# A two-step attention cycle with mixed score/maximum pairs, single-bank exponentials, and V, raw outputs and row maxima through DRAM

## The chip, the cores and the metric

One core of a Trainium2 chip. The metric is device microseconds of one execution. Engines: TensorE (PE) multiplies matrices into PSUM (eight banks of 128 partitions x 512 fp32), VectorE (DVE), ScalarE (ACT) and GpSimd (POOL) work on tiles, SP's queue issues most DMAs. Each engine runs its instructions in the order of its queue and waits on semaphores of the others.

## The reference

Two rounds of (multi-head attention block, then a dense block with Mish), each on a layer norm and added to x; all in fp32.

```python
B, S, D, H = 1, 2048, 512, 32        # head width 16; dense width F = 1792
def A(x, wqkv, wo):
    q, k, v = split(x @ wqkv)                    # [H, S, 16] each
    p = softmax(einsum("hqd,hkd->hqk", q, k) * 16 ** -0.5)
    return merge(einsum("hqk,hkd->hqd", p, v)) @ wo
def Bk(x, w1, b1, w2):
    h = x @ w1 + b1
    return (h * tanh(softplus(h))) @ w2
x = x + A(ln(x)); x = x + Bk(ln(x)); x = x + A(ln(x)); x = x + Bk(ln(x))
```

## The kernel before

Precision: where fp32 accuracy is wanted from fp32r matmuls, an operand is split in a high and a low part (`split_load`, `split_psum`), and `mm3` issues three matmuls for each product. Q and K are stacked in the partitions so that one matmul over 48 rows holds high and low parts (`KROWS`); two more rows (`MROWS` = 50) carry the negative row maximum in high and low parts against rows of ones in K. So a score matmul gives q.k - max directly, and the exponential needs no other operand. Even heads use partitions 0 to 49, odd heads 64 to 113 (`HALF`).

Stages, for each of two layers: q, k, v (`qkv`; q and k go to DRAM tiles `scr` and come back by head), attention, the output projection (`wo_parts`), the dense block (`mlp`). Attention runs over 8 groups of 4 heads; in a group over 4 blocks of 512 queries; in a block over 16 steps of 128 keys: 512 steps a layer, 32 blocks. A step has

- four score matmuls 50x128 by 50x512, into `sp` (two banks, two heads, item P, `pair`) or `ss` (one bank, item S, `single`), and the exponential of each PSUM tile into `p` (L312 for a pair, 1024 columns; L322 for a single, 512 columns);
- four maximum matmuls (item M twice, `max_mm`, tile `pm` of two banks for two heads) for a block that is 24 steps ahead (`AHEAD`), and for each M one reduction over 1024 columns on DVE (L265, tile `mxv`);
- two pv items (item v, `pv`, L339): half of the queries each, four heads side by side in the columns of the array, added up over the block in the bank `acc`. A fp32 matmul shows as two records here.

Every three steps follow the same cycle, and TensorE's instructions in attention are chained in that order (`pe`):

```python
CYCLE = ("PMSvv", "PMSvMPMSv", "PMSvvM")
```

At the end of a block of maxima DVE folds them (`max_fold`, L272, tile `nm`); TensorE transposes the fold (`nmt`), DVE splits it (`np`, L284 and L285), and eight DMAs on SP (L289) put the rows into the Q tiles `qs`. At the end of a block of pv ACT drains the bank (`ot`, L356); TensorE transposes it (`otp`), DVE takes the reciprocal of the sums and multiplies (`rc`, `o`, L367 and L368) into `ost`, four tiles that stay in SBUF. The four V tiles of a layer stay in SBUF too, and POOL builds from them the tile `va` of each group (L232 to L235). All these, the tiles of Q, K, `p` and the weights share one pool, `blk`, of 22 slots. PSUM: `pm` has two buffers of two banks, `sp` one of two banks, `ss` one, `acc` one.

The last 24 steps have no M items left; there the projection of the first 512 rows (`wo_parts`, transposes `op`, matmuls `wo`) is put between the steps. The weights `wo` and the first four tiles of w1 are loaded in the last group and split by POOL.

## Time and profile before

| | us |
|---|---|
| runs shown | 3944.41, 3948.99, 3965.48 (median 3948.99) |
| profiled execution, span | 3965.9 |
| first norm, q, k, v of layer 0 | 0 to 202 |
| attention, layer 0 | 202 to 1648.5 |
| rest of the projection, dense block, q, k, v of layer 1 (overlapping) | 1648.5 to 2194 |
| attention, layer 1 | 2194 to 3601.8 |
| rest of the projection, dense block | 3601.8 to 3966 |

The profiled execution's span stands at the time of the slowest of the three runs. In rows of stretches the columns are: start and end, length, then busy time and count for PE, PE's weight loads, DVE, ACT, POOL (with a filter on a line: that line's engine alone), the granted share of the TensorE clock, the busy share of the DMA engines, GB/s. In rows of the order of time: start, duration from the first to the last of the merged instructions, engine, line, operation, tiles, count, and in brackets the idle time before and what ended it. A TensorE record's duration counts its latency, so neighbours overlap; the distance of starts tells what one costs.

### The profile page before, as it was taken

What the parts mean: (1) busy time and instruction counts of PE and PEld (TensorE: products, weight loads), DVE (VectorE), ACT (ScalarE), POOL (GpSimd) and SP (SyncE); (2) the same over time, 40 slices, a digit from 0 to 9 for tenths busy, and PEclk for the clock granted to TensorE, in tenths of its full rate; (3) what the DMA queues carried; (4) which work ended last, traced back from release to release, by engine and by line L of the source; (5) the groups of instructions that cost most, each with busy time, mean ns of one, the idle gap of its engine ahead of it and who ended that gap; (6) DMA issues with size and microseconds to landing.
All of it is one profiled execution on the core that took longest, in us unless ns stands there. A gap on an engine that the chain in (4) does not pass through costs nothing.

```text
span 3965.9 us, 70422 instructions
## 1 busy us (share of the span) xinstructions
PE 3802.0 (96%) x29504; PEld 2090.7 (53%) x29504; DVE 3093.7 (78%) x3266; ACT 2517.8 (63%) x3445; POOL 494.2 (12%) x401
## 2 busy tenths in 40 slices
PE   7999999999999999999999999999999999999999
PEld 5744444444444444588776444444444444446887
DVE  5689989687988898466656799897998979965655
ACT  2177777576776777544431777776777767774444
POOL 1000000000000011254420000000000000204545
PEclk9999999697998999999999999998999989999999
DMA  6220111110010201100033201111110202101000
GB/s 186 107 34 10 26 18 18 17 18 18 18 28 8 34 12 44 53 7 22 22 123 128 34 7 29 18 18 18 18 30 6 34 2 34 34 23 59 11 11 22
DMA packets 65326, 134.58 MB, mean 34 GB/s; under 512 B 12272, under 2 KB 26608, under 8 KB 58864
## 3 DMA queue, kind: packets, MB, share of 16 engines
q1 hardware_dynamic: 42768, 89.17, 10.6%
q10 hardware_dynamic: 22240, 40.90, 2.9%
q8 instruction: 232, 3.80, 0.4%
q14 instruction: 86, 0.70, 0.1%
HBM read 85.99 MB, written 41.94 MB: 32 GB/s over the span
## 4 chain that ended last, share of the span: by engine, by line
PE 44%; DVE 4%; ACT 2%; POOL 1%; DMA 1%; issue 1%; POOLq 0%; DVEq 0%; ACTq 0%; SPq 0%
PE pv L339 13%; PE pm L261 9%; PE sp L311 6%; PE ss L321 4%; DVE mxv L265 2%; PE mo L133 1%; PE h L131 1%; PE h L133 1%; PE h L132 1%; PE mo L131 1%; PE mo L132 1%; ACT p L312 1%; POOL hb L532 1%; DVE al L533 1%; PE qk L131 1%
## 5 line engine op out<-in xcount | busy, mean ns | idle before, releaser
L265 DVE TENSOR_REDUCE mxv<-pm 128x2 f32<-128x1024 f32 x2048 | 2430.9, 1221 | 392.0 <-PE pm L261 380.6
L312 ACT ACTIVATE p<-sp 128x1024 f32<-128x1024 f32 x1366 | 1398.5, 1024 | 737.8 <-PE sp L311 642.8
L339 PE MATMUL pv<-p,va 128*32 128x256 f32 x16384 | 1221.2, 402 | 0.3
L261 PE MATMUL pm<-ks,qs 48*128 48x512 f32 x4096 | 954.0, 464 | 40.2 <-DVE mxv L265 38.0
L322 ACT ACTIVATE p<-ss 128x512 f32<-128x512 f32 x1364 | 809.2, 593 | 11.4 <-PE ss L321 11.4
L339 PEld LDWEIGHTS pv<-p,va 128*32 128x32 f32 x16384 | 403.3, 111 | 613.0 <-issue 488.2
L311 PE MATMUL sp<-qs,ks 50*128 50x512 f32 x2732 | 645.6, 467 | 69.6 <-ACT p L312 64.2
L261 PEld LDWEIGHTS pm<-ks,qs 48*128 48x128 f32 x4096 | 397.9, 192 | 449.4 <-issue 279.3
L321 PE MATMUL ss<-qs,ks 50*128 50x512 f32 x1364 | 561.2, 411 | 0.0
L311 PEld LDWEIGHTS sp<-qs,ks 50*128 50x128 f32 x2732 | 267.2, 190 | 400.3 <-ACT p L312 318.3
L232 POOL MEMSET va<- 128x2048 f32 x16 | 28.9, 1809 | 2390.8 <-ACT p L312 900.1
L321 PEld LDWEIGHTS ss<-qs,ks 50*128 50x128 f32 x1364 | 264.4, 194 | 90.5 <-ACT p L322 58.1
L529 POOL TENSOR_TENSOR hb<-hb,he 128x512 f32<-128x512 f32 x112 | 157.1, 1403 | 186.2 <-DVE he L526 179.4
L131 PE MATMUL mo<-w,ah 128*128 128x512 f32 x448 | 179.4, 400 | 0.8 <-DVE ah L531 0.7
L131 PE MATMUL h<-thm,w 128*128 128x512 f32 x448 | 176.0, 393 | 1.6 <-ACT hb L523 1.6
L132 PE MATMUL mo<-w,ah 128*128 128x512 f32 x448 | 177.3, 396 | 0.0
L532 POOL TENSOR_TENSOR hb<-hb,hr 128x512 f32<-128x512 f32 x112 | 160.1, 1430 | 136.4 <-DVE ah L531 115.4
L133 PE MATMUL h<-thm,w 128*128 128x512 f32 x448 | 175.6, 392 | 0.0
L132 PE MATMUL h<-tlm,w 128*128 128x512 f32 x448 | 175.2, 391 | 0.0
L533 DVE TENSOR_TENSOR al<-hb,ah 128x512 fp32r<-128x512 f32 x112 | 110.8, 989 | 81.9 <-POOL hb L532 81.9
L133 PE MATMUL mo<-w,al 128*128 128x512 f32 x448 | 163.7, 402 | 7.8 <-DVE al L533 7.8
L527 ACT ACTIVATE hr<-he 128x512 f32<-128x512 f32 x112 | 70.9, 633 | 156.9 <-DVE he L526 78.3
(168 smaller groups left out, 2777.2 us busy)
## 6 DMA issues: line engine op xcount, KB each, us to landing
scr<-pt ACTq DMA_DIRECT2D x64, 512.0 KB
qs<-scr SPq DMA_DIRECT2D x192, 128.0 KB
ks<-scr SPq DMA_DIRECT2D x192, 128.0 KB
qs<-np SPq DMA_DIRECT2D x512, 2.0 KB
x<-in_A_x_dram SPq DMA_DIRECT2D x7, 1024.0 KB
xs<-x SPq DMA_DIRECT2D x4, 1024.0 KB
x<-xs SPq DMA_DIRECT2D x4, 1024.0 KB
out_dram<-x SPq DMA_DIRECT2D x3, 1024.0 KB
```

The source lines that it names most:

```text
L131: pe(nc.tensor.matmul(acc, ah, bh, start=first and i == 0, stop=False))
L132: pe(nc.tensor.matmul(acc, ah, bl, start=False, stop=False))
L133: pe(nc.tensor.matmul(acc, al, bh, start=False, stop=last and i == n - 1))
L261: nc.tensor.matmul(pm[:, e], qs[u][rows, q0 : q0 + P], ks[u][rows, ts(n, 512)], start=True, stop=True)
L265: nc.vector.tensor_reduce(self.mxs[b][:, 2 * u : 2 * u + 2, qt, n], pm, axis=AX.X, op=ALU.max)
L311: self.pe(nc.tensor.matmul(sp[:, e], k, q, start=True, stop=True))
L312: nc.scalar.activation(self.pts[-1][:, 0:n], sp[:, 0:n], AF.Exp, scale=SCALE)
L321: self.pe(nc.tensor.matmul(sp, k, q, start=True, stop=True))
L322: nc.scalar.activation(self.pts[i // 3][:, 2], sp, AF.Exp, scale=SCALE)
L339: nc.tensor.matmul(acc[ts(h, VW), cols], va[:, kt, h, :], self.pts[j][:, e, cols], start=kt == 0 and half == 0, stop=kt == NKT - 1, skip_g ...
L529: nc.gpsimd.tensor_tensor(hb, hb, e, op=ALU.mult)
L532: nc.gpsimd.tensor_tensor(hb, hb, r, op=ALU.mult)
```

## The change

A cycle is now two steps long, written as one string; Q is a pair of scores in two separate banks, X a mixed pair (one score, one maximum, of heads in opposite row halves), M a pair of maxima as before, R a pair of scores in the banks that maxima used. The order of TensorE, and now of DVE's reductions and ACT's exponentials too, is chained (`Order`). PSUM is laid out once for the whole kernel: `s` three single banks (scores; q, k, v; hidden tiles), `n` two single banks (maxima of X; projection; transposes), `mx` one pair of banks (maxima of M), `acc` one.

Every exponential covers one bank (512 columns), 4 a step. For each step two maxima are reduced as one 1024-column reduction and two as single 512-column ones.

V is written to DRAM (`vscr`) as it is made and each group's `va` is loaded from there. A block's drained output goes to DRAM as it is (`raw`, `rawsum`); once per 512 queries `heads` loads the sums, takes the reciprocal, writes it out, spread over the 16 columns of a head, loads outputs and reciprocals with heads in the partitions, and multiplies and splits on DVE and POOL. `project` has no transposes. The row maxima are split on POOL, transposed by DVE in 32x32 pieces and go through DRAM into `qs`: four DMAs out, four in.

```diff
-CYCLE = ("PMSvv", "PMSvMPMSv", "PMSvvM")
+CYCLE = "QvXXvQMXvvXM"
+TAIL = "QRvvQRvv"
+    PS_BUFS = {"s": 3, "n": 2, "acc": 1}
     def pbank(tag, name):
-        if tag == "s":
-            return banks["s"].tile([P, 512], F32, tag=tag, name=name, bufs=3)
-        return ps.tile([P, 512], F32, tag=tag, name=name, bufs=1)
+        return ps.tile([P, 512], F32, tag=tag, name=name, bufs=PS_BUFS[tag])
+    def pwide(name):
+        return ps.tile([P, 2, 512], F32, tag="mx", name=name, bufs=1)
...
         def prep_v(self, g):
             va = b8([P, NKT, HG, VW], F32, f"va{self.l}{g}")
-            nc.gpsimd.memset(va, 0.0)
-            nc.gpsimd.memset(va[:, :, :, DH : DH + 1], 1.0)
-            for c in range(NCH):
-                nc.gpsimd.tensor_copy(va[:, ts(c, NCH), :, 0:DH], self.vall[c]...)
+            nc.sync.dma_start(va.rearrange("p t h w -> p (t h w)"), self.vscr[g].rearrange("p t n -> p (t n)"))
...
+        def max_pair(self):
+            b, qt, c = self.max_at(self.nm)
+            pm = pwide(f"pm{self.l}{self.nm}")
+            for h in range(2):
+                self.max_half(pm[:, h], b, h, qt, c)
+            self.order(nc.vector.tensor_reduce(self.mxs[b][:, 0:2, qt, c], pm, axis=AX.X, op=ALU.max))
+        def max_one(self, between=None):
+            h = 3 - self.nx % 2
+            pm = pbank("n", f"pn{self.l}{self.nx}")
+            self.max_half(pm, b, h, qt, c)
+            if between:
+                between()
+            self.order(nc.vector.tensor_reduce(self.mxs[b][:, h, qt, c : c + 1], pm, axis=AX.X, op=ALU.max))
...
         def max_fold(self, b):
+            nc.gpsimd.tensor_copy(nh[:, 0], nm)
+            nc.gpsimd.tensor_tensor(nh[:, 1], nm, nh[:, 0].bitcast(F32), op=ALU.subtract)
-            self.later.append((2, lambda: self.max_rows(b, nm)))
+            self.later.append((1, lambda: self.max_rows(b, nh)))
-        def max_rows(self, b, nm):
-            self.pe(nc.tensor.transpose(tp[0 : HG * NCH, 0:P], nm, ident))
-            nc.vector.tensor_copy(np_[:, 0], tp[0 : HG * NCH, 0:P])
-            nc.vector.tensor_tensor(np_[:, 1], tp[0 : HG * NCH, 0:P], np_[:, 0].bitcast(F32), op=ALU.subtract)
+        def max_rows(self, b, nh):
+            self.order(nc.vector.transpose(nt, nh.bitcast(F32).rearrange("p a r -> p (a r)")))
+            for j in range(NCH):
+                nc.sync.dma_start(rows[:, :, :, j, :]..., nt[32 * j : 32 * j + 32, :])
+            for h in range(HG):
+                nc.sync.dma_start(qs[h // 2][r : r + 2, ts(qb, CW)].bitcast(F32), rows[:, h]...)
...
-            nc.scalar.activation(self.pts[-1][:, 0:n], sp[:, 0:n], AF.Exp, scale=SCALE)
+            return lambda: self.order(nc.scalar.activation(self.pts[s][:, h], sp, AF.Exp, scale=SCALE))
+        def mixed(self):
+            f = self.score("s")
+            self.max_one(f)
...
         def pv(self, i):
+                    self.order(nc.scalar.activation(ot, self.accs.pop(b), AF.Copy))
+                    nc.sync.dma_start(self.sums[qb][ts(g, HG), :], ot[DH::VW, :])
+                    for h in range(HG):
+                        nc.sync.dma_start(self.raw[qb][ts(g * HG + h, DH), :], ot[h * VW : h * VW + DH, :])
...
+    def heads(att, c):
+        nc.sync.dma_start(sums, att.sums[c])
+        nc.vector.reciprocal(sums, sums)
+        nc.sync.dma_start(inv, sums[:, None, :].to_broadcast([H, DH, CW]))
+        nc.sync.dma_start(o, att.raw[c].rearrange("(k p) q -> p k q", p=P))
+        nc.sync.dma_start(r, inv.rearrange("h d q -> (h d) q").rearrange("(k p) q -> p k q", p=P))
+        for k in range(KT):
+            nc.vector.tensor_tensor(oh[:, k], o[:, k], r[:, k], op=ALU.mult)
+            nc.gpsimd.tensor_tensor(o[:, k], o[:, k], r[:, k], op=ALU.mult)
+            nc.vector.tensor_tensor(ol[:, k], o[:, k], oh[:, k].bitcast(F32), op=ALU.subtract)
...
-        order += [(m, c) for m in (1, 5, 2, 6, 3, 7) for c in range(NCH) if (m, c) not in order]
+        order += [(m, c) for m in (1, 5) for c in range(NCH) if (m, c) not in order]
+        order += [("v", c) for c in range(NCH)]
+        order += [(m, c) for m in (2, 6, 3, 7) for c in range(NCH)]
...
-        for i in range(4):
-            hooks[STEPS - GSTEPS + 8 + 2 * i] = lambda i=i: load_w1(i, hi="pool")
+        hooks[STEPS - 18] = lambda: behind(0)      # behind(c): heads(att, c)
+        hooks[STEPS - 12] = lambda: behind(1)
         for c in range(NCH):
             if c == 0:
+                behind(2)
+            if c == 1:
+                behind(3)
+            project(l, c, parts.pop(c), wot, x2s[c])
+            if c == 0:
+                for i in range(2):
+                    load_w1(i, hi="pool")
```

The dense block's sums `mo` take the two `n` banks and the wide `mx` tile instead of two wide tiles.

TensorE in the steady part of attention, before: tiles `pm` (maxima), `sp` and `ss` (scores), `pv`.

```order
L261 MATMUL pm_14749<-ks_12708,qs_12709 128x512 x2
L311 MATMUL sp_14753<-qs_12709,ks_12708 128x512 x2
L261 MATMUL pm_14758<-ks_12708,qs_12709 128x512 x2
L321 MATMUL ss_14762<-qs_13125,ks_13124 128x512
L339 MATMUL pv_14400<-p_14689,va_13867 32x256 x2
L339 MATMUL pv_14400<-p_14709,va_13867 32x256 x2
```

And after: `pn` is the single-bank maximum of an X item.

```order
L322 MATMUL sp_12891<-qs_10694,ks_10693 128x512 [waits Activation_49]
L242 MATMUL pn_12893<-ks_10693,qs_10694 128x512 [waits DVE_49]
L322 MATMUL sp_12897<-qs_10694,ks_10693 128x512 [waits Activation_49]
L242 MATMUL pn_12899<-ks_10693,qs_10694 128x512 [waits DVE_49]
L348 MATMUL pv_12611<-p_12815,va_10954 32x256 x4
L322 MATMUL sp_12908<-qs_10220,ks_10219 128x512 [waits Activation_49]
L322 MATMUL sp_12910<-qs_10220,ks_10219 128x512 [waits Activation_49]
L242 MATMUL pm_12914<-ks_10219,qs_10220 128x512 [waits DVE_49]
L242 MATMUL pm_12914<-ks_10219,qs_10220 128x512
```

The single score that had no partner is gone; a score and a maximum stand together, each waiting for another engine to free its bank.

DVE at the end of a block of maxima, before: the fold `nm`, then the reductions go on, and the split `np` of the transposed fold comes one reduction later.

```order
L265 TENSOR_REDUCE mxv_5768<-pm_6219 128x2 [waits PE_49]
L272 TENSOR_REDUCE nm_6223<-mxv_5768 128x16 [waits DVE_49]
L265 TENSOR_REDUCE mxv_6230<-pm_6231 128x2 [waits PE_49]
L284 CAST np_6248<-nmt_6246 16x128 [waits DMAHW4_49,DMAHW3_49,DMAHW5_49,DMAHW2_49,DMAHW6_49,DMAHW1_49,DMAHW7_49,DMAHW0_49,PE_49]
L285 TENSOR_TENSOR np_6248<-nmt_6246,np_6248 16x128 [waits DVE_49]
```

And after: `nt` is the transposed fold, `nh` the fold as POOL has split it.

```order
L260 TENSOR_REDUCE mxv_7009<-pm_7497 128x2 [waits PE_49]
L282 TENSOR_REDUCE nm_7501<-mxv_7009 128x16 [waits DVE_49]
L296 STREAM_TRANSPOSE nt_7506<-nh_7503 128x32 [waits DMAHW5_49,DMAHW4_49,DMAHW6_49,DMAHW3_49,Pool_49]
L275 TENSOR_REDUCE mxv_7530<-pn_7531 128x1 [waits PE_49]
L275 TENSOR_REDUCE mxv_7530<-pn_7537 128x1 [waits PE_49]
```

The transpose stands directly behind the fold whose POOL successor it waits for, with the next block's reductions behind it.

More of the change, by code (lines that the diff above doesn't have):

```diff
@@ new lines, in prep_v, with max_at, max_half @@
+            nc.sync.dma_start(va.rearrange("p t h w -> p (t h w)"), self.vscr[g].rearrange("p t n -> p (t n)"))
+            self.va[g] = va
+        def max_at(self, n):
+            b, i = divmod(n, NKT)
+            qt, c = divmod(i, NCH)
+            if b not in self.mxs:
+                self.mxs[b] = tmp.tile([P, HG, NCH, NCH], F32, tag="mxv", name=f"mxv{self.l}{b}")
+            return b, qt, c
+        def max_half(self, out, b, h, qt, c):
+            g, qb = divmod(b, NCH)
+            ks, qs = self.qk[g]
+            rows = slice(h % 2 * HALF, h % 2 * HALF + KROWS)
+            q0 = qb * CW + qt * P
+            self.order(
+                nc.tensor.matmul(
+                    out, qs[h // 2][rows, q0 : q0 + P], ks[h // 2][rows, ts(c, 512)], start=True, stop=True
+                )
+            )
@@ L537, in outp @@
             if f == 0:
-                obs[c] = [ps.tile([P, 2, 512], F32, tag="mx", name=f"mo{l}{c}{i}") for i in range(2)]
+                wide = pwide(f"mo{l}{c}")
+                obs[c] = [pbank("n", f"mo{l}{c}0"), pbank("n", f"mo{l}{c}1"), wide[:, 0], wide[:, 1]]
             ah, al = acts.pop((c, f))
@@ L653 @@
         if l == 0:
[L654 to L655 removed]
+            late = lambda: norm(x2s[last], f"q1{last}", tt, last, "n", True)
 TCKW = dict(schedule_with_timeline_sim=True)
```

436 lines of the change are left out of this document (186 added, 250 removed).

## The prediction

> **What bounds the kernel now.** I read the page first: share of each engine, the line of the granted clock, the costliest groups.
>
> ```profile
> span 3965.9 us, 70422 instructions
> PE 3802.0 (96%) x29504; PEld 2090.7 (53%) x29504; DVE 3093.7 (78%) x3266; ACT 2517.8 (63%) x3445; POOL 494.2 (12%) x401
> PEclk9999999697998999999999999998999989999999
> L265 DVE TENSOR_REDUCE mxv<-pm 128x2 f32<-128x1024 f32 x2048 | 2430.9, 1221 | 392.0 <-PE pm L261 380.6
> L312 ACT ACTIVATE p<-sp 128x1024 f32<-128x1024 f32 x1366 | 1398.5, 1024 | 737.8 <-PE sp L311 642.8
> L322 ACT ACTIVATE p<-ss 128x512 f32<-128x512 f32 x1364 | 809.2, 593 | 11.4 <-PE ss L321 11.4
> L339 PE MATMUL pv<-p,va 128*32 128x256 f32 x16384 | 1221.2, 402 | 0.3
> ```
>
> TensorE (PE) looks full, but its busy time counts latency, so I went on to the busy time by stretches: the two attention stages (first score to last output drain), then single blocks of 16 steps with the row-maximum instruction L265 alone.
>
> ```profile
> 202.00:1648.50 1446.50, 1392.81 (x12413) 637.46 (x12410) 1209.85 (x1154) 1050.25 (x1397) 47.75 (x58) 0.93 0.11 21
> 2194.00:3601.80 1407.80, 1352.83 (x12413) 622.53 (x12413) 1209.22 (x1154) 1050.26 (x1397) 48.71 (x58) 0.97 0.12 21
> 334.80:375.70 40.90, 37.26 (x32) 1.00 0.01 2
> 416.60:460.00 43.40, 39.06 (x34) 1.00 0.23 39
> 673.80:740.30 66.50, 40.17 (x34) 0.66 0.00 1
> 1246.10:1310.60 64.50, 39.54 (x34) 0.68 0.00 1
> ```
>
> The stages take 1446.5 + 1407.8 = 2854.3 us, 72% of the span. At full clock a block takes 40.9 or 43.4 us, with VectorE (DVE) 91% in reductions; in some blocks TensorE is granted two thirds of its clock and the block takes 65. The order of time on TensorE shows what a block is made of.
>
> ```profile
> 1000.91 0.50 PE L311 MATMUL sp<-qs,ks 50*128 50x512 f32 x2
> ...
> 1002.82 0.50 PE L261 MATMUL pm<-ks,qs 48*128 48x512 f32 x2
> 1003.16 0.40 PE L311 MATMUL sp<-qs,ks 50*128 50x512 f32 x2
> 1003.39 0.39 PE L261 MATMUL pm<-ks,qs 48*128 48x512 f32 x2
> 1003.63 0.39 PE L321 MATMUL ss<-qs,ks 50*128 50x512 f32 x1
> 1003.94 1.07 PE L339 MATMUL pv<-p,va 128*32 128x256 f32 x16
> 1004.94 0.50 PE L311 MATMUL sp<-qs,ks 50*128 50x512 f32 x2
> ...
> 1005.52 0.40 PE L321 MATMUL ss<-qs,ks 50*128 50x512 f32 x1
> 1005.85 0.64 PE L339 MATMUL pv<-p,va 128*32 128x256 f32 x8
> 1006.41 0.50 PE L261 MATMUL pm<-ks,qs 48*128 48x512 f32 x2
> ...
> 1008.33 0.50 PE L311 MATMUL sp<-qs,ks 50*128 50x512 f32 x2
> ```
>
> Starts count here, not durations. Two matmuls on opposite row halves (x2) start together and take one slot; a single takes a whole slot too. A slot is 0.34 us when it follows a pv, 0.23 inside a run, 0.32 before a pv; one pv item (x8: four heads, each in two passes) with the change back is 0.56, two are 1.00. Three steps hold 10 pairs, 4 singles and 6 pv items in four runs (MPMS-vv, PMS-v, MPMS-v, PMS-vv): 2.12 + 1.47 + 1.68 + 1.91 = 7.18 us, 2.39 a step. TensorE is the bound, with DVE close behind.
>
> **The change, part by part.**
>
> *The cycle.* Two steps become Q v XX v QMX vv XM. Every score or maximum matmul now has a partner, so 16 matmuls are 8 slots, in three runs instead of 2.7: (XMQ-v) 0.89 + 0.56, (XX-v) 0.66 + 0.56, (QMX-vv) 0.89 + 1.00 = 4.56 us, 2.28 a step. DVE keeps two wide reductions for two steps and gets four of 512 columns for the other two; ScalarE (ACT) gets eight exponentials of 512. Nearest rows, in order of time:
>
> ```profile
> 2109.77 1.23 DVE L265 TENSOR_REDUCE mxv<-pm 128x2 f32<-128x1024 f32 x1 [0.66 <-PE pm L261]
> 2110.91 0.68 DVE L126 TENSOR_TENSOR pt<-qk,pt 128x512 fp32r<-128x512 f32 x1
> 2111.50 1.22 DVE L265 TENSOR_REDUCE mxv<-pm 128x2 f32<-128x1024 f32 x1
> 3960.39 2.48 DVE L550 TENSOR_TENSOR x<-mo,x 128x512 f32<-128x512 f32 x4 [1.30 <-PE mo L133]
> 2031.26 1.07 ACT L125 ACTIVATE pt<-qk 128x512 fp32r<-128x512 f32 x2
> ```
>
> Back to back a wide reduction occupies DVE for 1.14 us (2110.91 - 2109.77), a 512-column read of PSUM for 0.59 to 0.60 (2111.50 - 2110.91; the four of L550). No 512 reduction is in the trace; its bounds are 0.57 (half a wide one) and 0.68 (its whole duration, no overlap). I take 0.595. Two steps: 2 x 1.14 + 4 x 0.595 = 4.66 us. ACT: the second of two 512 reads starts 1.07 - 0.60 = 0.47 after the first; with 0.02 for hand-overs eight are 3.9. So DVE becomes the bound, TensorE 2% behind. A block is 8 x 4.66 = 37.3.
>
> The Trainium skill (Perfetto Trace Analysis, Optimizing Scalar/DVE Operations) speaks against this split: it gives each DVE instruction on PSUM about 125 ns of access overhead and advises grouping on a saturated engine. The rows leave about 0.05 (twice 0.595 less 1.14). With the page's 125 ns on the 0.545 of data, an estimate from that page, a 512 reduction would cost 0.67 and the sum would be some 150 us higher; I hold to the rows.
>
> *Block borders.* Gone from TensorE and DVE: the transposes nmt and otp and their four DVE followers. In their place the fold is followed directly by a DVE transpose that waits for two small POOL operations on what the fold has just written.
>
> ```profile
> 1006.99 0.22 DVE L272 TENSOR_REDUCE nm<-mxv 128x16 f32<-128x64 f32 x1
> L235 POOL COPY va<-v x64: 396/400/403, 164.5 to 3383.6; 128x256 f32<-128x256 f32 x64
> L368 DVE TENSOR_TENSOR o<-otp,rc x64: 408/424/427, 257.1 to 3606.9; 128x256 f32<-128x256 f32 x64
> L289 SPq DMA_DIRECT2D qs<-np x512: 572/573/651, 156.4 to 3536.9; - x171
> ```
>
> DVE stands still for that: fold 0.22, two POOL operations (each at most the 0.40 of 256 columns, here 16), the transpose (at most 0.42), hand-overs: 0.5 to 1.5, I take 1.0. Behind the waiting transpose the next reductions queue, and behind those TensorE's X and M slots once the two narrow and one wide buffers are full. Block: 38.3; I add 1% for in-order coupling (today's cycle, from the P at 1000.91 to that at 1008.33, takes 7.42 against 7.18): 38.7.
>
> *Waits that go.* V, the outputs and their tiles leave the 22-slot pool: eight slots more for the exponentials. Today exponentials wait for a slot until a pv has read it, and TensorE then stands:
>
> ```profile
> 688.50 1.02 ACT L312 ACTIVATE p<-sp 128x1024 f32<-128x1024 f32 x1 [1.32 <-PE pv L339]
> 689.57 0.50 PE L311 MATMUL sp<-qs,ks 50*128 50x512 f32 x2 [1.15 <-ACT p L312]
> ```
>
> This is what makes 43.4 of 40.9, and the half-speed stretches begin at such places (block 673.8). With the stalls gone I expect the clock to stay up. What is late next is DVE itself.
>
> *Tail of 24 steps without maxima.* Four exponentials a step, 4 x 0.49 = 1.95 us (TensorE 1.88): 47 us. Now the last blocks cost as much as the others, with the first output projection among them:
>
> ```profile
> 1606.20:1648.50 42.30, 40.51 (x352) 18.09 (x351) 12.00 (x19) 28.89 (x40) 4.02 (x3) 1.00 0.01 1
> 1648.50:1693.30 44.80, 44.03 (x226) 36.33 (x225) 34.68 (x52) 13.60 (x21) 23.34 (x11) 1.00 0.37 129
> ```
>
> A stage becomes 30.5 blocks x 38.7 + 47 + 10 (first matmul, the last two pv steps, two reciprocals that stand among the reductions and wait for DMA) = 1237 us.
>
> *After attention.* All four projections now follow it: 48 more matmuls at 0.23 are +11, the 48 transposes op that go are about -5 (they share the 44.8 us above with 144 wo matmuls, 33, and 14 h). The chain sums, reciprocal, inverse, reload of the last quarter through DRAM hides under three projections, 33 us. POOL gets the splits of w100 and w101 and the multiplications of two quarters, some 20 us more ahead of the first hb; cover is 45 us of projection and five hidden tiles. I take +8 a layer, bounds 0 and +25.
>
> *V through DRAM, banks of mo, order of qkv.* Each V tile is written while 12 matmuls (2.8 us) and a set of maxima run; POOL's va copies go, off the path. TensorE's work before attention is the same. I put it at 0, bounds -5 and +10 a layer.
>
> *Sum* against the profiled execution: 3966 - 2854 + 2 x 1237 + 2 x 8 = 3602. The profiled span is that of the slowest run shown (3965.48); the median is 17 us lower. That scatter is of the size of the half-clock time, which I expect to go, so I carry nothing over: 3600.
>
> **The rivals.**
>
> *The clock falls as now.* The clocks of 0.93 and 0.97 mean 2 x (0.07 x 1446.5 + 0.03 x 1407.8) = 287 us at half speed. There a block is TensorE-bound, 2 x 36.5 = 73 us against 38.7, so the same 287 us would hold up the new kernel by 287 x (1 - 38.7/73) = 135: 3737. For it: the mix of matmuls is the same and TensorE still fills its time loosely. Against: the stalls that precede the falls go. The Trainium skill (TensorE: Matmul & The Clock Gate, Part 1) ties a fall to an idle window of some 3.4 us; the trace has falls next to idle times of 1.15, so the page would rule this rival out and the rows do not.
>
> *Narrow reductions do not overlap.* 2 x 1.22 + 4 x 0.68 = 5.16, block 42.3: 2 x 30.5 x 3.6 = +220, 3820. Against: L126 and L550 overlap on the same bank type.
>
> *Row maxima arrive late (slower).* They now go to DRAM and back: four writes, four reads, eight issues of 0.57 on SP (4.6 us) and two landings, behind the loads of the next heads. They are needed 8 steps (19 us) after the fold. It costs nothing until the two landings pass about 12 us, and makes the kernel slower than before from 18 (6 us x 61 borders = 366); at 20, 8 x 61 = 488: 4090. Against: today's eight issues and one landing within the same eight steps leave no DMA wait worth a row.
>
> *Mixed pairs do not run side by side* because each half waits on another engine: four slots more, 0.23 to 0.34 each, block 45 to 49: 3990 to 4230. Against: today's pairs take one slot also where their heads lie in different tiles.
>
> **How the numbers follow.** Forecast 0.71 (3535 to 3690: border 0.5 to 1.5, coupling 0 to 2%, after attention 0 to +25), clock 0.14, no overlap 0.05, late maxima 0.04, no pairing 0.03, the rest small mixtures. Range 3535 to 3745 takes in forecast and clock. Faster 0.93 (forecast, clock, no overlap, the mixtures), slower 0.05 (late maxima, most of no pairing), same 0.02; within 0.5% (20 us) this kernel's runs cannot tell, having 21 us of scatter.
>
> **What would show it.** Blocks of 38 to 39 us with DVE above 95% in them; narrow reductions 0.60 apart; a pair of sp and pn starting together; one DVE gap of a microsecond per block ahead of nt, with POOL as its end; PEclk 9 throughout attention; attention stages near 1240. I am wrong if TensorE waits for DMA at the first score of a block, or if the clock line keeps its sixes and sevens.

## The result, and the profile after

The changed kernel takes 3737.7 us (median of four runs, 3735.0 to 3746.6) where the kernel before, run on the same chips, took 3957.2 (four runs): ratio 0.948 (95% interval 0.943 to 0.953). That is faster, as forecast, but by 220 us and not by the 350 that 3600 us meant. The time happens to equal that of the rival with the falling clock, but the profile shows another cause. That it lies within the stated range of 3535 to 3745 us is luck: the range reached so far up for that rival alone, and the forecast's own part of it ended at 3690.

From the page of the changed kernel: span, engines, granted clock, the chain that ended last by line, and the costliest groups.

```profile
span 3733.7 us, 70993 instructions
PE 3518.1 (94%) x29056; PEld 1936.2 (52%) x29056; DVE 3096.8 (83%) x4150; ACT 2564.1 (69%) x4787; POOL 521.5 (14%) x465
PEclk8999999999999998899989999999999999888999
DVE mxv L275 29%; DVE mxv L260 28%; PE pv L348 3%; POOL hb L520 2%; PE sp L322 2%; DVE al L521 2%; PE qk L139 1%; POOL hb L517 1%; DVE he L512 1%; PE qk L141 1%; PE qk L140 1%; DVE ah L519 1%; DMA rall<-inv 1%; DVE he L514 1%; PE va L139 1%
L324 ACT ACTIVATE p<-sp 128x512 f32<-128x512 f32 x4096 | 2134.1, 599 | 348.0 <-PE pn L242 206.1
L275 DVE TENSOR_REDUCE mxv<-pn 128x1 f32<-128x512 f32 x2048 | 1323.1, 694 | 27.9 <-PE pn L242 27.1
L260 DVE TENSOR_REDUCE mxv<-pm 128x2 f32<-128x1024 f32 x1024 | 1260.9, 1231 | 78.5 <-PE pm L242 78.0
```

The chain now runs through VectorE's two kinds of reductions (57%). The clock is 9 through the middle of both attentions and 8 at their ends, behind them and among q, k and v of layer 1. The stretches say the same (columns as explained ahead of the prediction): the two attentions, one steady block, a stretch with the matmuls of one block near the end of attention, and the output projections behind it.

```profile
209.90:1464.90 1255.00, 1213.09 (x12194) 543.01 (x12194) 1182.79 (x1550) 1080.51 (x2081) 42.12 (x81) 0.98 0.20 42
2068.70:3325.50 1256.80, 1217.69 (x12194) 544.70 (x12194) 1184.87 (x1551) 1080.81 (x2081) 41.73 (x81) 0.98 0.20 42
253.60:291.90 38.30, 37.77 (x386) 16.93 (x386) 37.66 (x51) 33.83 (x66) 0.42 (x2) 1.00 0.38 75
1370.60:1417.80 47.20, 40.88 (x386) 18.04 (x382) 24.05 (x29) 36.20 (x71) 0.42 (x2) 0.89 0.37 117
1464.80:1527.60 62.80, 50.76 (x196) 39.44 (x196) 49.83 (x63) 1.20 (x2) 30.28 (x15) 0.89 0.50 154
```

A steady block is 38.3 us with VectorE busy 98% of it, at full clock. In TensorE's order of time, the score and the maximum of a pair start together:

```profile
700.63 0.50 PE L322 MATMUL sp<-qs,ks 50*128 50x512 f32 x1
700.63 0.50 PE L242 MATMUL pn<-ks,qs 48*128 48x512 f32 x1
```

In VectorE's, a wide reduction takes 1.13 us from start to start and two narrow ones 1.20; at the end of a block of maxima the transpose waits 0.60 us for GpSimd:

```profile
699.63 1.22 DVE L260 TENSOR_REDUCE mxv<-pm 128x2 f32<-128x1024 f32 x1
700.76 1.29 DVE L275 TENSOR_REDUCE mxv<-pn 128x1 f32<-128x512 f32 x2
701.96 1.22 DVE L260 TENSOR_REDUCE mxv<-pm 128x2 f32<-128x1024 f32 x1
...
578.04 0.22 DVE L282 TENSOR_REDUCE nm<-mxv 128x16 f32<-128x64 f32 x1
578.86 0.21 DVE L296 STREAM_TRANSPOSE nt<-nh 128x32 f32<-128x32 f32 x1 [0.60 <-POOL nh L288]
```

So the steady part is what was forecast, and the 132 us between this profile's 3734 and the sum of 3602 lie at the seams. Stage by stage against the forecast: up to the first score 209.9 us (202), attention 1255.0 and 1256.8 (1237 each), from there to layer 1's first score 603.8 (553.5), from layer 1's attention to the end 408.2 (372). Three places show in the waits. The first maxima, placed among q, k and v, wait for the reload of the Q and K rows:

```profile
76.00 0.79 PE L242 MATMUL pm<-ks,qs 48*128 48x512 f32 x1 [6.36 <-DMA ks<-scr]
82.08 0.79 PE L242 MATMUL pm<-ks,qs 48*128 48x512 f32 x1 [5.30 <-DMA qs<-scr]
91.69 0.89 PE L242 MATMUL pn<-ks,qs 48*128 48x512 f32 x2 [8.81 <-DMA qs<-scr]
```

In the last blocks, the reciprocals of the sums stand among the reductions and wait for DMA, TensorE waits behind them, and then an exponential waits 13.5 us for a pool slot that GpSimd's multiplication still reads:

```profile
1333.54 3.34 DVE L470 RECIPROCAL sums<-sums 32x512 f32<-32x512 f32 x1 [4.00 <-DMA sums<-rawsum]
1337.47 0.79 PE L242 MATMUL pn<-ks,qs 48*128 48x512 f32 x1 [6.75 <-DVE mxv L275]
1380.16 3.34 DVE L470 RECIPROCAL sums<-sums 32x512 f32<-32x512 f32 x1 [3.47 <-DMA sums<-rawsum]
1453.41 4.03 ACT L324 ACTIVATE p<-sp 128x512 f32<-128x512 f32 x8 [13.46 <-POOL oraw L481]
1454.06 0.79 PE L322 MATMUL sp<-qs,ks 50*128 50x512 f32 x1 [12.13 <-ACT p L324]
```

The last three blocks of a layer take 47.2, 44.6, 46.0 us (49.5, 43.2, 46.0 in layer 1). And in the projections (62.8 us, where 192 matmuls at 0.23 are 44) TensorE stands 12 us for a bank that VectorE's addition to x should free. The group of the first matmuls of a product, from 1455 to 1540 us:

```profile
L139 PE MATMUL wo<-wo,oh 128*128 128x512 f32 x64 | 27.7, 433 | 12.0 <-DVE x L496 12.0
```

VectorE's queue holds casts, statistics and multiplications there, and runs slower beside GpSimd. In its order of time, multiplications of two quarters:

```profile
1419.06 4.67 DVE L480 TENSOR_TENSOR oh<-oraw,rall 128x512 fp32r<-128x512 f32 x4 [18.52 <-DMA rall<-inv]
1455.05 1.28 DVE L480 TENSOR_TENSOR oh<-oraw,rall 128x512 fp32r<-128x512 f32 x2
```

Of the four of a quarter the first two take 1.28 us, since GpSimd joins during the second; all four take 4.67. The third and the fourth each end some 0.55 us behind a multiplication of GpSimd's (1422.05 behind 1421.49, 1423.74 behind 1423.19). That is what the Trainium skill (SBUF — State Buffer, SBUF: two separate sides) says of a shared port that is locked for a whole instruction; these rows agree.

### The profile page after: what moved, and what is told of

Same layout as the page of the kernel before. It is cut to its first block, busy times and chain, and to the rows that moved or that the text cites. A ratio compares the mean times of both kernels' runs of the same rounds, so it can differ in the third digit from the quotient of the medians.

```text
span 3733.7 us, 70993 instructions
## 1 busy us (share of the span) xinstructions
PE 3518.1 (94%) x29056; PEld 1936.2 (52%) x29056; DVE 3096.8 (83%) x4150; ACT 2564.1 (69%) x4787; POOL 521.5 (14%) x465
## 4 chain that ended last, share of the span: by engine, by line
DVE 67%; PE 17%; POOL 5%; DMA 4%; ACT 3%; issue 2%; SPq 0%; ACTq 0%; POOLq 0%; DVEq 0%
DVE mxv L275 29%; DVE mxv L260 28%; PE pv L348 3%; POOL hb L520 2%; PE sp L322 2%; DVE al L521 2%; PE qk L139 1%; POOL hb L517 1%; DVE he L512 1%; PE qk L141 1%; PE qk L140 1%; DVE ah L519 1%; DMA rall<-inv 1%; DVE he L514 1%; PE va L139 1%
## 5 line engine op out<-in xcount | busy, mean ns | idle before, releaser
L324 ACT ACTIVATE p<-sp 128x512 f32<-128x512 f32 x4096 | 2134.1, 599 | 348.0 <-PE pn L242 206.1
L275 DVE TENSOR_REDUCE mxv<-pn 128x1 f32<-128x512 f32 x2048 | 1323.1, 694 | 27.9 <-PE pn L242 27.1
L260 DVE TENSOR_REDUCE mxv<-pm 128x2 f32<-128x1024 f32 x1024 | 1260.9, 1231 | 78.5 <-PE pm L242 78.0
L322 PE MATMUL sp<-qs,ks 50*128 50x512 f32 x4096 | 1298.0, 450 | 27.0 <-ACT p L324 26.7
L322 PEld LDWEIGHTS sp<-qs,ks 50*128 50x128 f32 x4096 | 573.3, 185 | 745.8 <-ACT p L324 628.3
L242 PE MATMUL pn<-ks,qs 48*128 48x512 f32 x2048 | 825.0, 451 | 70.6 <-DVE mxv L275 53.2
L242 PE MATMUL pm<-ks,qs 48*128 48x512 f32 x2048 | 439.6, 423 | 22.8 <-DMA ks<-scr 16.7
L242 PEld LDWEIGHTS pn<-ks,qs 48*128 48x128 f32 x2048 | 366.9, 184 | 94.9 <-DVE mxv L275 76.6
L242 PEld LDWEIGHTS pm<-ks,qs 48*128 48x128 f32 x2048 | 195.1, 186 | 86.2 <-DMA ks<-scr 18.0
L133 ACT ACTIVATE pt<-qk 128x512 fp32r<-128x512 f32 x64 | 38.0, 598 | 194.6 <-PE qk L141 185.8
```

Source lines behind the costliest of these rows:

```text
L242: nc.tensor.matmul(out, qs[h // 2][rows, q0 : q0 + P], ks[h // 2][rows, ts(c, 512)], start=True, stop=True)
L260: self.order(nc.vector.tensor_reduce(self.mxs[b][:, 0:2, qt, c], pm, axis=AX.X, op=ALU.max))
L275: self.order(nc.vector.tensor_reduce(self.mxs[b][:, h, qt, c : c + 1], pm, axis=AX.X, op=ALU.max))
L322: nc.tensor.matmul(sp, ks[h // 2][rows, ts(kt, P)], qs[h // 2][rows, ts(qb, CW)], start=True, stop=True)
L324: return lambda: self.order(nc.scalar.activation(self.pts[s][:, h], sp, AF.Exp, scale=SCALE))
```

## The experiments

Unless said otherwise a kernel differs from the changed kernel (3737.7 us) by the edit shown; times are medians, and the runs of each kernel but those told of below lie within 14 us.

**The maxima among q, k, v (later maxima).**

```diff
-                        start = i + 3
+                        start = i + 8
+                    chained = chained or i >= start     # ahead of the maxima of a V tile
```

> Edit: the first row maxima of a layer begin with the V items (eight items after the last k/q row of part 0 is out) and not three items after it. Theory (the seams): TensorE, whose order is chained from the first maximum on, then finds ks and qs already loaded. In the changed kernel it stands 6.36 + 5.30 + 8.81 us for them in layer 0 and 6.76 + 3.56 + 8.55 us in layer 1, and runs for some 50 us a layer at a clock of about 0.8. So the start to the first score falls from 209.9 us to 185-200, layer 1's likewise by 10-20, and the time to 3700-3722. Rival (the loads are late whenever they are asked for, or the same work is only moved): the idle times reappear at other items and the time stays at 3730-3745.

3701.1 us, 36.6 less. The waits for DMA are gone from the stretch before attention; what is left of TensorE's waits from 60 to 192 us (us in total, times, longest):

```profile
PE va L139 <- ACT vst L426: 1.2, 1, 1.2
PE pm L242 <- DVE mxv L260: 0.5, 1, 0.5
```

The first score comes at 192 us, not 210, and layer 1's 586 us behind attention, not 604. The bare waits were 20.5 and 18.9 us; 36.6 of these 39.4 came back.

**The border.**

```diff
-            self.later.append((1, lambda: self.max_rows(b, nh)))
+            self.later.append((3, lambda: self.max_rows(b, nh)))
```

> Edit: the transpose of a block's row maxima stands one cycle of two steps later (3 ticks, not 1), so that GpSimd's copy and subtraction of the 16 maxima run beside reductions. Theory (VectorE bounds the steady part): the 0.6 us per block for which VectorE waits for GpSimd goes, blocks go from 38.3 to 37.7 us, and the time falls by 30 to 40 us to 3697-3710. Rival 1 (TensorE or ScalarE stands right behind VectorE, or the reductions wait for a bank anyway): blocks stay at 38.2-38.4 and the time at 3733-3745. Rival 2 (the rows of maxima then come late): blocks over 39 us.

3696.2 us, 41.5 less. VectorE goes from the fold to reductions, and the transpose finds its rows ready:

```profile
575.85 0.22 DVE L282 TENSOR_REDUCE nm<-mxv 128x16 f32<-128x64 f32 x1
575.99 1.28 DVE L275 TENSOR_REDUCE mxv<-pn 128x1 f32<-128x512 f32 x2
...
580.64 0.20 DVE L296 STREAM_TRANSPOSE nt<-nh 128x32 f32<-128x32 f32 x1
```

A block, as a stretch, is 37.6 us with VectorE busy 37.57:

```profile
784.90:822.50 37.60, 37.60 (x386) 17.04 (x386) 37.57 (x51) 33.83 (x66) 0.42 (x2) 1.00 0.03 6
```

0.7 us a block came back in full: VectorE is the bound, and nothing stood right behind it.

**Casts on ScalarE in the interlude.**

```diff
-                    load_w1(i, hi="dve")      # and load_w2(i, hi="dve")
+                    load_w1(i, hi="act")
```

> Edit: after attention the nine weight casts of w1 (2 to 6) and w2 (0 to 3) go from VectorE to ScalarE, which is idle there for 47 us. Theory (VectorE is crowded in the interlude and the additions to x stand behind casts and statistics): the projections go from 62.8 us to 48-55, the MLP's first matmul from 75 us after attention to 60-68, and the time falls by 8-15 us a layer to 3708-3724. Rival (the chain of sums, reciprocal, inverse and reload through DRAM sets the interlude, or ScalarE's casts come ahead of its copies of the normalised rows): the first matmul of the MLP stays at 72-78 us and the time at 3730-3745.

3727.1 us, 10.6 less in the median (3724.1 to 3735.0, so about as much as the runs differ; the profiled run gained 0.5). The projections stay at 62 us and the first hidden tile comes 71 us behind attention, not 75. Between the two theories, closer to the rival: the casts alone do not set the interlude.

**The last blocks, in five runs.** First the reciprocals behind the last reduction.

```diff
-        nc.vector.reciprocal(sums, sums)
+        att.order(nc.vector.reciprocal(sums, sums))
```

> Edit: the reciprocals of the sums join VectorE's written order, so the two that run during attention stand behind the last reduction. Theory: the two of them cost 3.34 us each and 4.00 and 3.47 us of waiting for the sums, with TensorE idle 6.75 and 6.22 us at those places and at a low clock after it; blocks 29 and 30 fall from 47.2 and 44.6 us to 38-42, and the time by 8-15 us a layer: 3707-3722. Rival: the chain that starts at the reciprocal then ends later, the exponentials wait longer for a slot and the first projection starts later; what blocks 29 and 30 gain, block 31 and the projections give back, and the time stays within 3728-3745.

3728.1 us, 9.6 less. Blocks 29 and 30 take 38.3 and 35.8 us, but the last one 61.8: the rival's way, most of the wait moved on. The next run adds later loads of x, two slots more:

```diff
-            hooks[STEPS - 20 + i] = lambda i=i: load_res(i)
+            hooks[STEPS - 2 + i] = lambda i=i: load_res(i)
```

> Edit: the reciprocals stand behind the last reduction (as in the run before this that did that alone) and the two loads of x for the residual come at the end of attention, not 20 steps before, so that two of the 22 slots are free while the first two quarters of the output are put together. Theory (exponentials of the last block wait for a slot that the raw output of quarter 0 holds: 61.8 and 61.5 us for the last block where the reciprocals stood last): the last block falls to 32-40 us, and the time from 3728 to 3665-3690. Rival (the slots taken are given to other tiles and the wait stays, or the loads of x are late for the additions behind the projections): last block over 50 us or projections over 70 us, time 3715-3740.

3716.7 us, last block 54.2: by both numbers the rival, for the wait stays, though the last block is 7.6 us shorter. In ScalarE's order, the last block of layer 0 with the reciprocals last:

```profile
1448.64 4.03 ACT L324 ACTIVATE p<-sp 128x512 f32<-128x512 f32 x8 [29.32 <-POOL oraw L481]
```

and with late x, the one long wait now in two:

```profile
1421.58 4.03 ACT L324 ACTIVATE p<-sp 128x512 f32<-128x512 f32 x8 [11.23 <-POOL oraw L481]
1448.26 4.03 ACT L324 ACTIVATE p<-sp 128x512 f32<-128x512 f32 x8 [8.77 <-POOL oraw L481]
```

An earlier chain (`heads` cut in two, `ahead` for sums, reciprocal and inverse, the rest as before):

```diff
+        hooks[STEPS - 22] = lambda: ahead(0)
+        hooks[STEPS - 20] = lambda: ahead(1)
         hooks[STEPS - 18] = lambda: behind(0)
         hooks[STEPS - 12] = lambda: behind(1)
+        hooks[STEPS - 10] = lambda: ahead(2)
```

> Edit: as the run with late x, and the chain of sums, reciprocal and inverse is a function of its own that starts earlier than the loads of the raw outputs: for quarters 0 and 1 right behind the last reduction, for quarter 2 ten steps before the end of attention (not behind it), for quarter 3 at the end. Theory (the projections take 62 us and not 44 because quarters 2 and 3 only start their chains through DRAM at the end and TensorE is idle between them): the projections take 46-54 us, the MLP's first matmul starts 60-68 us after attention and not 75, and the time is 10-25 us below that of the run with late x. Rival (VectorE's casts and statistics set it, not the chain): projections stay at 58-63 us, and the time within 5 us of that run.

3718.0 us, last block 54.3, projections 62 and 64 us: the theory failed and the rival's numbers came, an earlier start buys nothing. That left the slots. My next reading was that a slot is handed on as soon as its last reader has been written down in the program, though that reader may still wait for a DMA. So the multiplications were moved behind the last exponential:

```diff
-        hooks[STEPS - 18] = lambda: behind(0)      # loads and multiplications
-        hooks[STEPS - 12] = lambda: behind(1)
+        hooks[STEPS - 18] = lambda: fetch(0)       # loads alone
+        hooks[STEPS - 12] = lambda: fetch(1)
+        hooks[STEPS - 1] = lambda: behind(0)       # multiplications alone
+        hooks[STEPS] = lambda: behind(1)
```

> Edit: as the early chain, but the raw outputs and inverses of quarters 0 and 1 are only loaded during the last 18 steps; their multiplications (which read the slots for the last time) are written behind the last exponential, and the loads of x come 40 steps before the end. Theory (the pool hands its 22 slots round in the order in which the program gives them back, so a slot given back by an instruction that still waits for a DMA stops the exponential that gets it next; slots are not short): no exponential gets such a slot, the last block falls from 54 to 33-38 us, and the time from 3717 to 3670-3700, a few us of it given back by multiplications behind attention. Rival (the pool is simply full): the last block stays over 48 us and the time at 3705-3725.

3682.0 us. The last block takes 30.8 us, 16 steps of 1.92, with TensorE busy throughout (the stretch of that block):

```profile
1401.90:1432.70 30.80, 30.80 (x311) 13.98 (x311) 7.59 (x7) 28.78 (x59) 7.03 (x4) 1.00 0.72 213
```

This run also takes fewer slots during the last steps (four fewer than the changed kernel, two fewer than the run with the early chain), so a last one takes them all early (`oh` and `ol` are allocated in `fetch`, the loads of x stand behind attention):

> Edit: as the run with arithmetic last, but all four slots of each of the first two quarters (raw output, inverse, high and low part) are taken when the loads are written, as in the run with the early chain, and the loads of x come behind attention, so that during the last steps as many slots are taken as there, 20 of 22 by count. Only what is handed back differs: nothing that still waits for a DMA. Theory (order in which slots are handed back): no exponential waits for GpSimd, the last block takes 31-34 us and the run 3675-3695. Rival (the pool is full): the last block takes 45-55 us, the exponentials wait for a slot, and the run takes 3705-3730.

3689.0 us, last block 30.8 again, no wait on GpSimd. With as many slots taken as in the run with the early chain, only what is handed back differs; the order of handing back made the wait, not a full pool. Of the 47 us that the two last blocks gain on late x, some 12 are given back: the multiplications now stand behind attention (first hidden tile 86 and 82 us behind it, with late x 76 and 75).

**A shorter chain.** As arithmetic last, and

```diff
-        sums = t512("he", f"sums{l}{c}")[0:H]
-        nc.sync.dma_start(inv, sums[:, None, :].to_broadcast([H, DH, CW]))
+        sums = t512("he", f"sums{l}{c}")[:, 0:P]     # 128 x 128
+        nc.sync.dma_start(inv.rearrange("h (a q) -> (h a) q", q=P), sums)
...
+        for k in range(KT):
+            nc.sync.dma_start(r[:, k], inv[ts(k, n), None, :].to_broadcast([n, DH, CW]))
```

> Edit: as the run before it, and the chain is shorter: the sums are read as 128 x 128 and not 32 x 512 for the reciprocal (3.34 us now), the inverse is written once (64 KB) and spread over the 16 rows of a head when it is read, not when it is written (1 MB written, 1 MB read now). Theory (the projections wait for the chain of the last quarter, 30 us from the last product to the first multiplication): that chain takes 17-24 us, the projections 46-56 us in place of 62, and the time is 10-28 us below that of the run before it. Rival (VectorE's queue of casts, statistics and additions sets the projections): the chain gets shorter, the projections stay at 58-63 us, and the time within 6 us of that run.

3661.6 us, 20.4 below arithmetic last. The reciprocal of the same 16384 sums costs little more than a quarter, in VectorE's order:

```profile
1453.06 0.94 DVE L470 RECIPROCAL sums<-sums 128x128 f32<-128x128 f32 x1
```

and the projections, as a stretch, take 57.7 us:

```profile
1435.30:1493.00 57.70, 49.66 (x198) 39.01 (x195) 49.98 (x72) 1.20 (x2) 34.36 (x20) 0.91 0.53 166
```

Between the two theories: the time fell as the chain's theory says, but the chain of the last quarter, from the last product to the first multiplication, takes 26.5 us and not 17 to 24 (36.2 with arithmetic last, 29.9 in the changed kernel). The projections fell less than it says, since they still wait 8.0 us for VectorE's additions to x.

**All together.** Arithmetic last, later maxima, transpose later and casts on ScalarE; then with the short chain and three banks for the first transposes (`norm(x2s[0], ..., "s")`).

> The changed kernel with the seams mended together: arithmetic last, later maxima, transpose one cycle later, casts on ScalarE. Theory (the four losses lie in different places and add): -36 (later maxima), -41 (transpose), -5 to -10 (casts) below the run with arithmetic last alone: 3585-3625 us. Rival (they overlap, a wait taken away in one place comes back in another): 3630-3670.

3599.5 us (3594.8 to 3601.7), ratio 0.912 (0.908 to 0.916): 82.5 below arithmetic last, where 36.6, 41.5 and 5 to 10 had been added up. The losses add, to within 6 us.

> As the run with the seams mended, with the short chain and with three banks, not one, for the transposes of the first normalised rows after attention (TensorE waits 6.1 + 1.9 + 1.4 us for VectorE's copies there). Theory: 10-28 us a run for the chain and 8-14 for the banks, so 3550-3605 us, at or below the 3600 us that was forecast for the change. Rival: VectorE sets the interlude, and the time is within 8 us of that run.

3577.5 us (3574.1 to 3579.6), ratio 0.906 (0.902 to 0.910), the fastest kernel here. Its attention is the same stretch in both layers:

```profile
194.90:1397.00 1202.10, 1200.69 (x12194) 544.59 (x12194) 1163.54 (x1541) 1081.00 (x2081) 32.47 (x74) 1.00 0.19 40
```

**Do mixed pairs run side by side?**

```diff
-            h = 3 - self.nx % 2
+            h = 2 + self.nx % 2
```

> Edit: the narrow maxima take the heads 2 and 3 in the other order, so that the score and the maximum of a mixed pair read the same half of TensorE's rows (heads 2 and 2, then 3 and 3) and not different ones. The amount of work is the same. Theory (two products on different halves of the rows run side by side and cost one slot of 0.234 us): four pairs per two steps each cost a slot more, TensorE needs 4.56 + 0.94 = 5.5 us per two steps and passes VectorE's 4.7; a block takes 43-47 us in place of 38.3, and the run 4030-4280 us. Rival (the pairs did not run side by side in the first place, or TensorE has that much room): blocks stay within 38-39 us and the time within 3725-3760.

3999.9 us (two runs), 262 more, and 1.2% above the kernel before (0.4 to 2.0%). Blocks take 41.3 us, not 43 to 47, and VectorE now waits for TensorE. Its waits from 300 to 1300 us:

```profile
DVE mxv L275 <- PE sp L322: 51.4, 168, 0.3
```

The reason for the smaller price is in TensorE's order of time, first an XX run, then a part of the run XMQ:

```profile
699.16 0.50 PE L322 MATMUL sp<-qs,ks 50*128 50x512 f32 x2
699.50 0.40 PE L242 MATMUL pn<-ks,qs 48*128 48x512 f32 x2
699.83 0.64 PE L348 MATMUL pv<-p,va 128*32 128x256 f32 x8
...
702.87 0.40 PE L242 MATMUL pn<-ks,qs 48*128 48x512 f32 x1
702.88 0.40 PE L322 MATMUL sp<-qs,ks 50*128 50x512 f32 x1
```

The program has the four matmuls of XX as score and maximum of head 2, then score and maximum of head 3. Here the two scores start together and then the two maxima: a matmul can start ahead of an earlier one that lies in the other half, and pairs form across items, not within the item as I had expected. So XX still costs two slots, 0.67 us (699.16 to 699.83) as in the changed kernel. In each of the other two runs one half now has four matmuls and the other two, and the run takes four slots where it took three: XMQ 1.14 us (702.53 to 703.67) for 0.95 (700.63 to 701.58 in the changed kernel). That is two slots more in two steps, some 0.4 us, not four and 0.94: TensorE's sum goes from 4.56 to about 4.95, and 5.16 were measured (41.3 / 8). Of the 262 us the 56 steady blocks make 56 x 3.0 = 168; most of the rest is at the ends of attention, where blocks 29 and 30 take 76 and 55 us in layer 0 at a lower clock.

**What V through DRAM does alone**, on the kernel before: V's tiles and GpSimd's copies leave, and nothing else changes.

```diff
-            nc.gpsimd.memset(va, 0.0)                      # and the copies from vall
+            nc.sync.dma_start(va.rearrange("p t h w -> p (t h w)"), self.vscr[g].rearrange("p t n -> p (t n)"))
```

> The kernel before with one part of the change: V goes through DRAM (the four tiles of all V and GpSimd's copies into va leave), so that the 22-slot pool has four slots more during attention; the cycle of three steps, the wide exponentials and the transposes stay. Theory (before's blocks of 43.4 us and its stretches at half clock come from exponentials that wait for a slot in the pool, with TensorE idle 1.15 us beside them): the slow blocks go to 40.9 us, the stretches at half clock go, attention falls from 1446 and 1408 us to 1310-1340 each, and the run to 3760-3840 us. Rival 1 (the clock falls for another reason, the slot wait only moves): attention stays above 1380 us in both layers and the run within 3900-3980. Rival 2 (the first V arrives late): a single wait of 5-10 us a layer at the start of attention.

3815.5 us (3810.4 to 3838.4), ratio 0.967 (0.961 to 0.972): two thirds of the whole gain. Attention takes 1346.8 and 1354.7 us, a little more than the theory's 1310 to 1340. The stretches at half clock are gone; the blocks of 43.4 us are not, so the slots do not make them. They come regularly, as every third block, so I put them down to the three-step cycle. Is it the slots or GpSimd's copies? Holding four tiles of V's size tells:

```diff
+            v = b8([P, NCH, D], F32, f"v{l}{c}")           # for each of four c
+            nc.gpsimd.memset(v[:, 0, 0:1], 0.0)
...
+                    nc.gpsimd.tensor_copy(keep, t[:, 0, 0:1])      # in the last group
```

> Edit: the kernel before with V through DRAM, and four tiles of the size of the four V tiles are held from the V stage to the last group with one column each written and read, so that the pool has as many slots for the exponentials as before the change, while V still comes by DMA and GpSimd's copies into va stay away. Theory (the four slots are what V through DRAM gave): exponentials wait for pv again, stretches at half clock return, and the time goes from 3815 back to 3900-3990. Rival (it was GpSimd's copies and their contention, or V's place in the program): no such waits, the time stays at 3800-3840.

3817.8 us (3809.4 to 3852.8), and no verdict: the reads that were to end the holding had been drawn ahead, so nothing was held. In GpSimd's order:

```profile
101.07 0.43 POOL L237 COPY keep<-v 128x1 f32<-128x1 f32 x3
```

The second time they need the last group's `va` (`tensor_tensor(keep, t[:, 0, 0:1], va[:, 0, 0, 0:1])`):

> Edit: as the run before it, but the reads that give the four held tiles back need the V tile of the last group as well, so that they cannot be drawn ahead (in the run before it they ran at 101 to 105 us, which gave the slots back before attention: it held nothing). Theory (the four slots are what V through DRAM gave): exponentials wait for pv again, TensorE stands 1.15 us at a time, stretches at half clock return, and the time goes from 3815 back to 3880-3990. Rival (GpSimd's copies or V's place in the program, not the slots): no such waits, time 3800-3840.

3985.9 us (ten runs, 3937.9 to 4013.2), ratio to before 1.006 (0.999 to 1.012): all of it is lost again. In GpSimd's order, those reads now run at the end of attention:

```profile
1398.34 0.61 POOL L237 TENSOR_TENSOR keep<-v,va 128x1 f32<-128x1 f32 x4 [1292.80 <-DMA va<-vscr]
```

TensorE's waits for exponentials from 300 to 1300 us, in the kernel before:

```profile
PE sp L311 <- ACT p L312: 27.3, 27, 1.2
```

with V through DRAM:

```profile
PE sp L305 <- ACT p L306: 0.6, 2, 0.3
```

and that run's granted clock over the whole span:

```profile
PEclk9999999999999999999999999999999999999999
```

with the slots held:

```profile
PE sp L309 <- ACT p L310: 28.0, 26, 1.2
```

and its granted clock:

```profile
PEclk9989989999998999999998899996989999999999
```

Four slots, some 27 waits of at most 1.2 us in a thousand, and with them the half clock: shown by giving the slots and taking them back. That the waits pull the clock down, and not something else that the slots bring, is read from the order in time. In the kernel before, TensorE's order:

```profile
698.12 0.50 PE L311 MATMUL sp<-qs,ks 50*128 50x512 f32 x2 [1.15 <-ACT p L312]
```

and the stretches up to 698.7 us and from there on, with the granted clock behind the counts:

```profile
681.60:698.70 17.10, 14.48 (x133) 6.78 (x132) 13.90 (x14) 10.66 (x14) 0.00 (x0) 1.00 0.00 1
698.70:777.20 78.50, 75.62 (x417) 31.84 (x419) 41.80 (x41) 34.80 (x46) 0.00 (x0) 0.50 0.06 10
```

All eight falls from 300 to 1300 us begin like this one, within 1.3 us behind the end of such a wait; but eight more waits of that length, at full clock in the same stretch, are followed by no fall, and what decides is not shown.

## Why the prediction was right or wrong

- **Cycle, right.** DVE's two-step sum 4.66 us, block 38.3 plus coupling 38.7: measured 38.27. Wide 1.13, narrow 0.60 (taken: 1.14, 0.595). The rival of narrow reductions that do not overlap fell, and with it the 0.67 estimated from Perfetto Trace Analysis (Optimizing Scalar/DVE Operations) in the Trainium skill: the rows disagree. TensorE's place 2% behind could be tested only from above: at 37.6 us a block it still does not hold VectorE up.
- **Border, right in kind.** "I take 1.0", bounds 0.5 to 1.5: the transpose alone waits 0.60 and taking it away gives 0.7 a block.
- **Waits that go, right but for one sentence.** The slots that V frees were counted there and are worth 150 us by themselves; all the rest of the change brings some 80. In the steady blocks the cycle alone gains more than that (41.7 us on average with V through DRAM, 38.3 here, some 210 us over 61 blocks), and the seams take most of it back. The "0" for V through DRAM holds only beside the slots. Wrong was "this is what makes 43.4 of 40.9": with no such wait left, blocks of both lengths remain.
- **Clock.** It stays up in the steady part, as forecast, so the rival of 3737 was not what happened. It falls at the seams, where TensorE stands. Neither of the two signs of being wrong appeared, no wait for DMA at the first score of a block and no sixes or sevens of the clock: they watched the steady part, and the miss is at the seams. In the kernel before and with the slots held, waits of at most 1.2 us are enough: the idle window of 3.4 us in TensorE: Matmul & The Clock Gate (Part 1) of the Trainium skill does not describe these falls.
- **Row maxima late, not seen.** No row of TensorE's waits in attention names their DMA.
- **Tail, wrong.** 1.95 us a step is right (1.92 where nothing disturbs). The failed step is "+ 10 (... two reciprocals that stand among the reductions and wait for DMA)": I saw the reciprocals and priced them as two short waits. They, and the slots handed back early, cost 33 us in layer 0 (1255 against 1222 with arithmetic last) and 38 in layer 1 (1257 against 1219), made up in part by blocks 0.4 us shorter than forecast. "V, the outputs and their tiles leave the pool: eight slots more" was true until the outputs came back in eight tiles in the last 18 steps.
- **After attention, wrong.** "+8 a layer, bounds 0 and +25": measured +58 and +44 against before. The step that failed is "hides under three projections, 33 us". The chain itself is 30 us (sums out at 1465, inverse in at 1494.7), but its multiplications then need until 1512 beside GpSimd, and VectorE's queue, with casts and statistics among additions to x, holds TensorE 12 us, another 7 us before the first hidden tile, and the clock at 0.89. Of the +58, 18 belong to the next point.
- **Order of qkv, wrong.** "I put it at 0, bounds -5 and +10 a layer": the order puts the first maxima 3 items behind the last row of K, in a chained queue; 37 us in all (run with later maxima). I had compared TensorE's work and not asked what the moved items wait for.

The 132 us by which this profile exceeds the sum are then: 36 from the maxima's place (18 ahead of each attention), 71 from the tail (33 and 38), 68 more after attention (32 and 36 beyond the +8), less 33 for an attention that is otherwise shorter than forecast (26 of them the blocks) and 10 for the rest of the stretch before attention. Of the first, 37 came back by one edit; of the tail, 56 net (3737.7 to 3682.0), since multiplications moved behind attention and made the interludes longer. The 20 us of the short chain mostly make that good: its two stretches behind attention take 603 and 401 us, against 604 and 408 in the changed kernel, so of the 68 it brings back only some 8. What stays open is the rest of the interlude: in the fastest kernel 579 us pass between the attentions, not 553.5, with TensorE busy 49 of the 58 us of projections, and that part was not taken further.

## What to carry to other kernels

Price a steady loop from start-to-start distances, then price its two ends separately: for every moved item ask which transfer it now stands in front of, and on an in-order queue who stands behind it. In a pool of slots, a tile is as expensive as what its last reader waits for; write the last reader down late, and count what a freed tile gives before crediting a new loop with the gain. An experiment that holds a resource must show in its trace that it held it.

## What the runs showed of the hardware that I had not expected

- TensorE fell to half clock within 1.3 us behind waits of 1.15 us, some 10 us apart, and stayed there for 3 to 78 us (kernel before, 300 to 1300 us). With the waits gone it ran at full clock from 13 and 26 us behind the first score to the end of the two attentions, 1333 and 1329 us.
- Matmuls on opposite row halves can pair across items, and one can start ahead of an earlier one of the other half: written score, maximum of one half, score, maximum of the other, they took two slots, 0.67 us.
- In these two rows a reciprocal is paid by columns: 3.34 us for 32 x 512, 0.94 for 128 x 128, the same 16384 values.
